# The first heads of a fused attention and soft-MoE kernel: how the first row of maxima travels, and what order the start-up work stands in

## The chip, the cores and the metric

One Trainium2 chip, one of its cores. The metric is device microseconds of one execution, the median of several runs. A profiled execution shows every instruction of the core's engines: PE (matrix products), PEld (its weight loads), DVE (VectorE), ACT (ScalarE), POOL (GpSimd), SP (which issues most transfers), and 16 DMA engines that carry the transfers.

## The reference

Attention over 4 x 8 heads of 768 positions and 64 dimensions, in which a query sees only the keys with its own hash bucket, and then a soft mixture of experts on the result:

```
q_bits = (einsum('bhsd,dk->bhsk', q, proj) > 0); k_bits likewise     # 6 bits each
mask   = q_bucket[:, :, :, None] == k_bucket[:, :, None, :]
scores = where(mask, (q @ k^T) / sqrt(64), -1e9)
attn   = softmax(scores);  attn_out = attn @ v
x      = attn_out as [3072, 512];  logits = x @ phi                  # 32 slots
slots  = softmax over tokens (logits)^T @ x; per expert relu(. @ w1) @ w2
out    = softmax over slots (logits) @ that
```

All values are 32-bit floats.

## The kernel before

The 32 heads go through one software pipeline, in pairs that share a load. For a pair, `load` brings q and k, transposed, into `raw` (two transfers of 384 KB; one buffer, so the next pair's load waits until this one has been read). `split_hi` (ACT) writes a rounded copy of `raw` into `w4` and `split_lo` the rest beside it, so that one product over 128 rows adds the high and low parts. `bits` multiplies `raw` by the projection and turns the signs into rows `bt` that push scores of unequal buckets far down. `w4` and `bt` also have one buffer each.

A head's operands are put together in one of three tiles `XY0`, `XY1`, `XY2` (names XY_133, XY_134, XY_135 in the order lists below) by transfers from SBUF to SBUF, all called `move`: `spread_y` (384 KB, the high parts of Y), `spread_bits` (four small ones from `bt`), `spread_l` (192 KB), `spread_x` (384 KB and 192 KB). The first head of all writes its Y rows directly. `first_y` zeroes some rows of a tile on GpSimd and sends rows of ones into it.

For each head `smax` (12 products, smx) finds the maximum of every query's row with 9 reductions on DVE; `shift` makes the shift `mz` of them (three tiny DVE operations m, mz, mz); `shift_rows` turns it into a row, row 64 of X and Y; `scores` (24 products, st) computes the scores again, with that row inside, and ACT takes their exponential into three tiles `pt`; `acc` (GpSimd) sums them, `av` multiplies them by v (24 products). Heads overlap: while head h is in `scores`, head h+1 is in `smax`.

`shift_rows` for every head but the first: PE transposes `mz` in one product, ACT copies the 12 x 128 result to `mr`, and SP sends it by one small transfer into row 64 of X and Y. For the first head, 24 products of one row each put the values on partition 64, and ACT and DVE copy them into the tile.

`keep_warm` issues products whose result nobody reads.

The order is a list, not a scheduler's choice: each step is entered by `at(when, f, ...)` with a time in slots, `WHEN` holds the times relative to a head, `FIRST` overrides single steps by absolute time, and the list is sorted. Each engine then runs its instructions in that order. SP's queue is in order too: a transfer that waits for its data holds up all that stand behind it.

Of the kernel before, what the change touches and what calls it, by code (L numbers as in the profile page):

```python
# [9 lines left out]
F32 = mybir.dt.float32  # L10
F32R = mybir.dt.float32r
AF = mybir.ActivationFunctionType
ALU = mybir.AluOpType
# [5 lines left out]
P = 128  # L19
NT = S // P  # L20
# [11 lines left out]
ROW = 64  # L32
# [39 lines left out]
 'batch_share': 27.6,  # L72
 'load_weights': 4.18}

FIRST = {('load', 4): 4.476,
 ('bits', 2): 1.288,
 ('split_hi', 2): 0.833,
 ('split_lo', 2, 0): 1.029,
 ('split_lo', 2, 1): 2.366,
 ('spread_y', 2): 1.587,  # L80
 ('spread_bits', 2): 1.668,
 ('spread_l', 2): 2.667,
 ('spread_x', 2): 3.34,
 ('smax', 1, 0, 0): -1.746,
 ('smax', 1, 0, 1): -1.169,
 ('smax', 1, 1, 0): 0.452,
 ('smax', 1, 1, 1): 0.57,
 ('smax', 1, 2, 0): 1.478,
 ('smax', 1, 2, 1): 1.593,
 ('smax', 1, 3, 0): 2.035,  # L90
 ('smax', 1, 3, 1): 2.061,
 ('smax', 1, 4, 0): 2.241,
 ('smax', 1, 4, 1): 2.696,
 ('smax', 1, 5, 0): 2.774,
 ('smax', 1, 5, 1): 3.433,
 ('one_sum', 30): 189.395,
 ('one_log', 30): 188.431,
 ('one_fold', 3): 189.992,
# [49 lines left out]
def lsh_attention_soft_moe(  # L148
# [11 lines left out]
    nc = tc.nc  # L160
# [35 lines left out]
    st = [dict() for _ in range(BH)]  # L196
# [21 lines left out]
    load(0)  # L218
    nc.sync.dma_start(out=pre[:, C_ID + 64:], in_=cst[:, C_ID:C_FD])
    phs = cp.tile([P, H, NS], F32, name="phs")  # L220
    for a in range(2):
        nc.sync.dma_start(out=phs[a * D:(a + 1) * D], in_=phi.rearrange("(h d) s -> d h s", d=D))

# [6 lines left out]
    ident = ident_r.bitcast(F32)  # L230
# [9 lines left out]
    p_st = ps_stack.enter_context(tc.tile_pool(name="p_st", bufs=3, space=PSUM))  # L240
    p_av = ps_stack.enter_context(tc.tile_pool(name="p_av", bufs=1, space=PSUM))
    p_mi = ps_stack.enter_context(tc.tile_pool(name="p_mi", bufs=2, space=PSUM))
    names = {p_sm: "smx", p_st: "st", p_mi: "mi"}
# [23 lines left out]
    def first_y(i):  # L267
        for ts in (Ys, Xs):
            nc.gpsimd.memset(ts[i][64:96].bitcast(F32), 0.0)
        for ts in (Ys, Xs)[i == 0:]:  # L270
            nc.gpsimd.dma_start(out=ts[i][ROW:ROW + 1, 1].bitcast(F32), in_=row)

# [16 lines left out]

    def split_lo(h, x):  # L290
        w = st[h]["w4"]
        (nc.vector if h else nc.gpsimd).tensor_tensor(out=w[:, 2 * x + 1], in0=st[h]["raw"][:, x], in1=w[:, 2 * x], op=ALU.subtract)  # L292

    def move(dst, src, eng=nc.sync):

        eng.dma_start(out=dst.bitcast(F32), in_=src.bitcast(F32))  # L296
# [10 lines left out]
    def spread_l(h):  # L307
        s = st[h]
        r = 64 * (h % 2)
        move(s["Y"][96:128], s["w4"][r:r + 32, 1:3])  # L310


    def spread_x(h):
        s = st[h]
        s["X"] = Xs[h % N_Y]
        r = 64 * (h % 2)
        move(s["X"][0:64], s["w4"][r:r + 64, 0::3])
        move(s["X"][96:128], s["w4"][r + 32:r + 64, 1:3])

    def over(out, pt, rows):  # L320
        nc.vector.tensor_scalar(out=out, in0=pt[rows, 0:HC], scalar1=con[rows, C_TH:C_TH + 1],  # L321
# [66 lines left out]

    def shift_rows(h):
        s = st[h]  # L390
        if h == 0:
            for t0, n in ((0, 4), (4, 2)):
                cols = slice(t0 * P, (t0 + n) * P)
                r = ROW
                for o, x, pool, copy in ((0, s["X"], p_mi, nc.scalar.copy),
                                         (NT, s["Y"], p_st, nc.vector.tensor_copy)):
                    pt = pool.tile([P, 512], F32, name=names[pool])
                    for t in range(n):
                        nc.tensor.matmul(pt[r:r + 1, t * P:(t + 1) * P], s["mz"][:, o + t0 + t:o + t0 + t + 1], ident,
                                         start=True, stop=True)  # L400
                    copy(x[r:r + 1, 0, cols], pt[r:r + 1, 0:n * P])
            return
        pt = p_mi.tile([P, 512], F32, name="mi")
        nc.tensor.transpose(pt[0:2 * NT, 0:P], s["mz"], ident)  # L404

        mr = mp.tile([2 * NT, P], F32R, name="mr", bufs=1)
        nc.scalar.copy(mr, pt[0:2 * NT, 0:P])  # L407
        move(s["XY"][ROW:ROW + 1, 0].rearrange("o y (t p) -> o (y t) p", p=P), mr)
# [306 lines left out]
    def at(when, f, *args):  # L715
        key = (f.__name__, *(a for a in args if isinstance(a, int)))
        plan.append((FIRST.get(key, when), len(plan), (f, *args)))

    first_y(0)
    for i in range(1, N_Y):  # L720
        at(-NT - 5 + i, first_y, i)
    at(-14, keep_warm, 10, True)
    at(-6.5, bits_rest)
    at(-13.9, bits_copy)
    at(-11, copy_ident)
    at(-2.6, keep_warm, 3, True)
    at(-2, keep_warm, 3, True)
    for h in range(BH):
        s0, x = NT * h, h % 2
        if x == 0:  # L730
            if h > 0:
                at(s0 + WHEN["load"], load, h)
            at(s0 + WHEN["bits"], bits, h)
            at(s0 + WHEN["split_hi"], split_hi, h)
            for n in range(2):
                at(s0 + WHEN["split_lo"][n], split_lo, h, n)
        for n, f in enumerate((spread_y, spread_bits, spread_l, spread_x)):
            at(s0 + WHEN["spread"][x][n], f, h)
        at(s0 + WHEN["load_v"][x], load_v, h)
        for n in range(2 * NT):  # L740
            at(s0 + WHEN["smax"][x][n], smax, h, n // 2, n % 2)
            at(s0 + WHEN["scores"][x][n], scores, h, n // 2, n % 2)
        at(s0 + WHEN["shift"][x], shift, h)
        at(s0 + WHEN["shift_rows"][x], shift_rows, h)
        for j in range(NT // 2):
            lone = h == BH - 1 and j == NT // 2 - 1
# [19 lines left out]
    last, h = NT * BH, BH - 1  # L766
# [62 lines left out]
    for x in range(2):  # L829
        pt = p_mi.tile([P, 512], F32, name="mi")[:, 0:2 * P]  # L830
        for k in range(2):
            nc.tensor.matmul(pt[:, k * P:(k + 1) * P], run_x[:, (2 * x + k) * P:(2 * x + k + 1) * P], fold,
                             start=True, stop=True)
# [176 lines left out]
```

## Time and profile before

| | us |
|---|---|
| median of 3 runs (523.57 to 529.93) | 524.46 |
| the profiled execution's own time | 524.46 |
| its span, first to last instruction | 522.4 |

The profiled execution took as long as the median run; 2.06 us of its time lie around the span. Mean granted TensorE clock over the span: 0.987 of full speed. In the page's lines a row is start, duration, engine, line, operation, output <- input, count, and in brackets how long the engine had been idle and what released it. In tables by stretch, each engine has its busy time, then come the granted clock (PEclk, 1.00 is full speed), the busy share of the DMA engines and GB/s.

### The profile page before, as it was taken

What the parts mean: (1) busy time and instruction counts of PE and PEld (TensorE: products, weight loads), DVE (VectorE), ACT (ScalarE), POOL (GpSimd) and SP (SyncE); (2) the same over time, 40 slices, a digit from 0 to 9 for tenths busy, and PEclk for the clock granted to TensorE, in tenths of its full rate; (3) what the DMA queues carried; (4) which work ended last, traced back from release to release, by engine and by line L of the source; (5) the groups of instructions that cost most, each with busy time, mean ns of one, the idle gap of its engine ahead of it and who ended that gap; (6) DMA issues with size and microseconds to landing.
All of it is one profiled execution on the core that took longest, in us unless ns stands there. A gap on an engine that the chain in (4) does not pass through costs nothing.

```text
span 522.4 us, 9095 instructions
## 1 busy us (share of the span) xinstructions
PE 499.2 (96%) x3164; PEld 284.3 (54%) x3164; DVE 369.3 (71%) x703; ACT 246.6 (47%) x463; POOL 326.8 (63%) x223
## 2 busy tenths in 40 slices
PE   7968999999999999999999999999999999999992
PEld 4544555555555555556554555565555555553562
DVE  6574877787878787777787788787777885464233
ACT  4144536464646454545454545454644545422232
POOL 9246767676739776767488785856588767411200
PEclk9789999999999999999999999999999999999998
DMA  5747475758585657575765757676636366879967
GB/s 126 188 98 188 116 196 173 193 168 197 169 197 168 178 143 203 152 210 143 217 149 167 183 175 178 188 181 182 146 101 154 73 156 234 319 286 352 410 275 293
DMA packets 39777, 99.59 MB, mean 191 GB/s; under 512 B 7458, under 2 KB 13732, under 8 KB 39732
## 3 DMA queue, kind: packets, MB, share of 16 engines
q1 hardware_dynamic: 39540, 98.94, 66.3%
q8 instruction: 25, 0.41, 0.3%
q14 instruction: 20, 0.16, 0.1%
q0 software_dynamic: 192, 0.08, 0.1%
HBM read 52.76 MB, written 6.29 MB: 113 GB/s over the span
## 4 chain that ended last, share of the span: by engine, by line
PE 70%; DVE 10%; SPq 7%; DMA 6%; POOL 2%; issue 2%; ACT 1%; DVEq 0%; ACTq 0%; POOLq 0%
PE st L421 20%; PE av L449 19%; PE smx L370 13%; SPq L296 7%; DMA XY<-bt 4%; PE qs L933 3%; DVE w L292 3%; PE qh L851 3%; DVE mx L376 3%; PE mi L461 2%; PE mi L476 2%; POOL acc L438 1%; PE mi L328 1%; DMA w<-w 1%; DMA XY<-w 1%
## 5 line engine op out<-in xcount | busy, mean ns | idle before, releaser
L438 POOL TENSOR_TENSOR acc<-acc,pt 128x768 f32<-128x768 f32 x125 | 238.8, 1911 | 39.4 <-ACT pt L425 27.1
L425 ACT ACTIVATE pt<-st 128x512 f32<-128x512 f32 x288 | 162.0, 595 | 97.2 <-PE st L421 90.8
L421 PE MATMUL st<-XY 128*128 128x512 f32 (+1 forms) x768 | 183.7, 347 | 0.0
L376 DVE TENSOR_REDUCE mx<-smx 128x1 f32<-128x512 f32 x192 | 130.8, 687 | 54.1 <-PE smx L370 53.8
L449 PE MATMUL av<-pt,v 128*64 128x384 f32 x768 | 145.3, 499 | 0.0
L370 PE MATMUL smx<-XY 96*128 96x512 f32 (+1 forms) x384 | 126.6, 375 | 9.9 <-DVE mx L376 5.4
L421 PEld LDWEIGHTS st<-XY 128*128 128x128 f32 x768 | 123.7, 191 | 21.1 <-issue 10.6
L370 PEld LDWEIGHTS smx<-XY 96*128 96x128 f32 x384 | 70.1, 191 | 74.4 <-DVE mx L376 26.1
L432 POOL TENSOR_TENSOR acc<-pt 128x768 f32<-128x768 f32 x32 | 58.6, 1830 | 63.8 <-ACT pt L425 63.8
L449 PEld LDWEIGHTS av<-pt,v 128*64 128x64 f32 x768 | 46.5, 136 | 62.7 <-issue 57.5
L373 DVE TENSOR_REDUCE mx<-smx 128x2 f32<-128x512 f32 x96 | 65.6, 683 | 4.3 <-PE smx L370 4.1
L292 DVE TENSOR_TENSOR w<-raw,w 128x768 fp32r<-128x768 f32 x30 | 41.2, 1373 | 3.7 <-ACT w L288 3.7
L468 DVE RECIPROCAL sm<-sm 128x128 f32<-128x128 f32 x45 | 39.6, 910 | 0.0
L288 ACT CAST w<-raw 128x768 fp32r<-128x768 f32 x32 | 25.1, 831 | 19.5 <-DMA XY<-w 9.7
L453 ACT COPY avs<-av 128x384 f32<-128x384 f32 x32 | 15.3, 478 | 37.2 <-PE av L449 37.2
L407 ACT CAST mr<-mi 12x128 fp32r<-12x128 f32 x31 | 7.9, 255 | 49.2 <-PE mi L404 44.6
L321 DVE TENSOR_SCALAR bt<-mi,con 128x384 fp32r<-128x384 f32 x15 | 10.1, 677 | 25.3 <-DMA XY<-bt 9.6
L607 POOL TENSOR_TENSOR dl<-lacc,dl 64x384 f32<-64x384 f32 x3 | 3.0, 999 | 25.6 <-ACT dl L606 25.6
L513 DVE TENSOR_TENSOR xq<-mi,r 128x256 f32<-128x256 f32 x45 | 17.3, 412 | 0.4 <-PE mi L511 0.4
L328 PE MATMUL mi<-raw,pb 128*32 128x384 f32 x128 | 15.2, 517 | 0.1
L933 PE MATMUL qs<-w 128*32 128x256 f32 x232 | 15.2, 382 | 0.0
L511 PE MATMUL mi<-ident,avs 128*128 128x128 f32 x90 | 14.8, 273 | 0.0
(173 smaller groups left out, 339.4 us busy)
## 6 DMA issues: line engine op xcount, KB each, us to landing
w<-w SPq DMA_DIRECT2D x61, 512.0 KB
XY<-w SPq DMA_DIRECT2D x63, 384.0 KB
raw<-qk SPq DMA_DIRECT2D x32, 384.0 KB
XY<-w SPq DMA_DIRECT2D x64, 192.0 KB
v<-vt SPq DMA_DIRECT2D x32, 192.0 KB
out<-w SPq DMA_DIRECT2D x12, 512.0 KB
xq<-w SPq DMA_DIRECT2D x3, 512.0 KB
XY<-bt SPq DMA_DIRECT2D x62, 19.5 KB
```

Source lines behind the costliest of these rows:

```text
L292: (nc.vector if h else nc.gpsimd).tensor_tensor(out=w[:, 2 * x + 1], in0=st[h]["raw"][:, x], in1=w[:, 2 * x], op=ALU.subtract)
L296: eng.dma_start(out=dst.bitcast(F32), in_=src.bitcast(F32))
L370: nc.tensor.matmul(pt[:, o:o + b - a], s["Y"][0:96, 0, t * P:(t + 1) * P], s["Y"][0:96, 1, a:b], start=True, stop=True)
L373: nc.vector.tensor_reduce(out=mx[:, n - 1:n + 1], in_=pt.rearrange("p (a x) -> p a x", a=2), axis=AX.X, op=ALU.max)
L376: nc.vector.reduce_max(out=mx[:, n:n + 1], in_=pt, axis=AX.X)
L421: nc.tensor.matmul(pt[:, o:o + b - a], x[:, 1, i * P:(i + 1) * P], x[:, 0, a:b], start=first, stop=not first)
L425: nc.scalar.activation(s["P", i // 2][:, 512 * u:512 * u + 512], pt, AF.Exp, scale=D ** -0.5)
L432: nc.gpsimd.tensor_tensor(out=s["acc"], in0=pr[:, 0:S], in1=pr[:, S:2 * S], op=ALU.add)
L438: eng.tensor_tensor(out=s["acc"], in0=s["acc"], in1=pr[:, a * S:(a + 1) * S], op=ALU.add)
L449: nc.tensor.matmul(s["av"][64 * c:64 * c + 64, 0:HC], s["v"][:, i, :], pr[:, o + c * HC:o + (c + 1) * HC], start=(i == 0), stop=(i == NT - 1))
L468: nc.vector.reciprocal(out=rs[:, k * P:(k + 1) * P], in_=rs[:, k * P:(k + 1) * P])
L933: nc.tensor.matmul(po[32 * j:32 * j + 32], hTs[g][:, f, 32 * j:32 * j + 32], wt[1, x, 2 * g + f // 4, j][:, (f % 4) * HM:(f % 4 + 1) * HM] ...
```

## The change

Four things, all in the first two pairs of heads; from the third pair on every engine runs the same instructions in the same order.

- The first head's row is transposed, copied to `mr` and sent by SP as for the other heads. The 24 one-row products and four copies go, and two groups of three `keep_warm` products.
- The second head's `smax` stands ahead of the first head's `scores`, instead of alternating with them; the third head's last parts stand later.
- GpSimd's queue issues the first head's `spread_l` and `spread_x` (three moves, 768 KB), which SP issued; `split_lo` of the second pair goes from DVE to GpSimd; the second and third heads' rows of ones come later.
- The second pair's `load` stands behind the second head's moves, and these behind the first head's row; `bits`, `split_hi` and the spreads of the second pair move to match.

```diff
-FIRST = {('load', 4): 4.476,
- ('bits', 2): 1.288,
- ('split_hi', 2): 0.833,
...
+ ('load', 2): -1.8,
+ ('spread_l', 1): -2.05,
+ ('spread_x', 1): -2.1,
...
     def first_y(i):
         for ts in (Ys, Xs):
             nc.gpsimd.memset(ts[i][64:96].bitcast(F32), 0.0)
+
+    def first_rows(i):
         for ts in (Ys, Xs)[i == 0:]:
             nc.gpsimd.dma_start(out=ts[i][ROW:ROW + 1, 1].bitcast(F32), in_=row)
...
-        (nc.vector if h else nc.gpsimd).tensor_tensor(out=w[:, 2 * x + 1], in0=st[h]["raw"][:, x], in1=w[:, 2 * x], op=ALU.subtract)
+        (nc.vector if h > 2 else nc.gpsimd).tensor_tensor(out=w[:, 2 * x + 1], in0=st[h]["raw"][:, x], in1=w[:, 2 * x], op=ALU.subtract)
...
-        move(s["Y"][96:128], s["w4"][r:r + 32, 1:3])
+        move(s["Y"][96:128], s["w4"][r:r + 32, 1:3], nc.sync if h else nc.gpsimd)
...
-        move(s["X"][0:64], s["w4"][r:r + 64, 0::3])
-        move(s["X"][96:128], s["w4"][r + 32:r + 64, 1:3])
+        eng = nc.sync if h else nc.gpsimd
+        move(s["X"][0:64], s["w4"][r:r + 64, 0::3], eng)
+        move(s["X"][96:128], s["w4"][r + 32:r + 64, 1:3], eng)
...
     def shift_rows(h):
         s = st[h]
-        if h == 0:
-            for t0, n in ((0, 4), (4, 2)):
-                cols = slice(t0 * P, (t0 + n) * P)
-                r = ROW
-                for o, x, pool, copy in ((0, s["X"], p_mi, nc.scalar.copy),
-                                         (NT, s["Y"], p_st, nc.vector.tensor_copy)):
-                    pt = pool.tile([P, 512], F32, name=names[pool])
-                    for t in range(n):
-                        nc.tensor.matmul(pt[r:r + 1, t * P:(t + 1) * P], s["mz"][:, o + t0 + t:o + t0 + t + 1], ident,
-                                         start=True, stop=True)
-                    copy(x[r:r + 1, 0, cols], pt[r:r + 1, 0:n * P])
-            return
...
     first_y(0)
+    first_rows(0)
     for i in range(1, N_Y):
         at(-NT - 5 + i, first_y, i)
+        at((-12.5, -3.52)[i - 1], first_rows, i)
     at(-14, keep_warm, 10, True)
     at(-6.5, bits_rest)
     at(-13.9, bits_copy)
-    at(-11, copy_ident)
-    at(-2.6, keep_warm, 3, True)
-    at(-2, keep_warm, 3, True)
+    at(-12.52, copy_ident)
```

SP's transfers before, from the second head's first move on (raw is the second pair's load here, bt the bits, v the first head's v; XY_135 is the third head's tile):

```order
L296 DMA XY_134<-w_155 64x2x768
L296 DMA XY_133<-w_155 32x2x768
L201 DMA raw<-qk 128x768 x2
L296 DMA XY_134<-bt 13x384 x2
L296 DMA XY_134<-bt 12x384 x2
L296 DMA XY_133<-w_155 64x2x768
L296 DMA XY_133<-w_155 32x2x768
L296 DMA XY_134<-w_155 64x2x768
L296 DMA XY_134<-w_155 32x2x768 x2
L278 DMA v_87<-vt 128x384
L296 DMA XY_135<-w_278 64x2x768
```

And now, to the same place (mr is the first head's row):

```order
L309 DMA XY_134<-w_153 64x2x768
L309 DMA XY_134<-bt 13x384 x2
L309 DMA XY_134<-bt 12x384 x2
L309 DMA XY_133<-mr 1x12x128
L309 DMA XY_134<-w_153 64x2x768
L309 DMA XY_134<-w_153 32x2x768 x2
L291 DMA v_87<-vt 128x384
L211 DMA raw<-qk 128x768 x2
L309 DMA XY_135<-w_292 64x2x768
```

The load moved from ahead of the second head's bits to behind that head's moves, the row stands ahead of those moves, and the first head's three moves are gone from this queue.

PE's products from the last maxima of the first head on, before (XY_133 is the first head, XY_134 the second):

```order
L370 MATMUL smx<-XY_133 128x512
L249 MATMUL av<-pt_83,ones 32x128 x3
L399 MATMUL mi<-ident,mz 1x128 x4
L399 MATMUL st<-ident,mz 1x128 x4
L399 MATMUL mi<-ident,mz 1x128 x2
L399 MATMUL st<-ident,mz 1x128 x2
L249 MATMUL av<-pt_83,ones 32x128 x3
L370 MATMUL smx<-XY_134 128x512
L370 MATMUL smx<-XY_134 128x256
L421 MATMUL st<-XY_133 128x512 x2
```

And now, from the same product:

```order
L384 MATMUL smx<-XY_133 128x512
L384 MATMUL smx<-XY_134 128x512
L384 MATMUL smx<-XY_134 128x256 x2
L406 MATMUL mi<-ident,mz 12x128
L384 MATMUL smx<-XY_134 128x512 x2
L384 MATMUL smx<-XY_134 128x256 x2
L384 MATMUL smx<-XY_134 128x512 x2
L423 MATMUL st<-XY_133 128x512 x2
```

The transposition of the shift stands behind the second head's first two maxima tiles, and that head's tiles run ahead of the first head's scores.

POOL's work before, from the second tile's zeroing to the first sum:

```order
L269 MEMSET XY_134 32x2x768 x2
L271 DMA XY_134<-acc_84 1x16x48 x2
L292 ISA
L292 TENSOR_TENSOR w_155<-raw,w_155 128x768 x2
L265 CAST ident<-pt_82 128x128
L269 MEMSET XY_135 32x2x768 x2
L271 DMA XY_135<-acc_84 1x16x48 x2
L432 TENSOR_TENSOR acc_84<-pt_81 128x768
```

And now:

```order
L280 MEMSET XY_134 32x2x768 x2
L305 ISA
L305 TENSOR_TENSOR w_153<-raw,w_153 128x768 x2
L276 CAST ident<-pt_82 128x128
L284 DMA XY_134<-acc_84 1x16x48 x2
L309 DMA XY_133<-w_153 32x2x768
L309 DMA XY_133<-w_153 64x2x768
L309 DMA XY_133<-w_153 32x2x768
L280 MEMSET XY_135 32x2x768 x2
L284 DMA XY_135<-acc_84 1x16x48 x2
L305 TENSOR_TENSOR w_292<-raw,w_292 128x768 x2
L434 TENSOR_TENSOR acc_84<-pt_81 128x768
```

The rows of ones moved behind the subtraction, three moves stand ahead of the third tile's zeroing, and the second pair's subtraction ahead of the first sum.

More of the change, by code (lines that the diff above doesn't have):

```diff
@@ L73 @@
  'load_weights': 4.18}
-FIRST = {('load', 4): 4.476,
- ('bits', 2): 1.288,
- ('split_hi', 2): 0.833,
[L78 to L95, printed above, removed]
+FIRST = {('smax', 2, 2, 1): 5.76,
+ ('smax', 2, 2, 0): 5.75,
+ ('smax', 2, 1, 1): 5.7,
+ ('smax', 2, 1, 0): 5.66,
+ ('smax', 2, 0, 1): 5.65,
+ ('smax', 2, 0, 0): 5.6,
+ ('load', 2): -1.8,
+ ('spread_l', 1): -2.05,
+ ('spread_x', 1): -2.1,
+ ('spread_x', 0): -12.04,
+ ('load', 4): 4.476,
+ ('bits', 2): 3.4,
+ ('split_hi', 2): 3.3,
+ ('split_lo', 2, 0): 3.45,
+ ('split_lo', 2, 1): 3.46,
+ ('spread_y', 2): 3.5,
+ ('spread_bits', 2): 3.6,
+ ('spread_l', 2): 4.2,
+ ('spread_x', 2): 4.3,
+ ('smax', 1, 0, 0): -2.3,
+ ('smax', 1, 0, 1): -2.29,
+ ('smax', 1, 1, 0): -2.28,
+ ('smax', 1, 1, 1): -2.1,
+ ('smax', 1, 2, 0): -2.05,
+ ('smax', 1, 2, 1): -2.0,
+ ('smax', 1, 3, 0): -1.99,
+ ('smax', 1, 3, 1): -1.9,
+ ('smax', 1, 4, 0): -1.8,
+ ('smax', 1, 4, 1): 0.62,
+ ('smax', 1, 5, 0): 0.63,
+ ('smax', 1, 5, 1): 1.2,
  ('one_sum', 30): 189.395,
```

## The prediction

> **What bounds the kernel now.** I read the page's first part, then busy time by stretches of the start, then the chain of waits backwards from where the start ends.
>
> ```profile
> PE 499.2 (96%) x3164; PEld 284.3 (54%) x3164; DVE 369.3 (71%) x703; ACT 246.6 (47%) x463; POOL 326.8 (63%) x223
> 9.00:21.70 12.70, 10.74 (x49) 6.13 (x49) 7.97 (x15) 1.32 (x3) 7.44 (x7) 0.73 0.69 171
> 21.70:30.00 8.30, 4.69 (x27) 2.99 (x26) 4.60 (x8) 3.63 (x6) 0.58 (x1) 1.00 0.50 116
> 30.00:39.40 9.40, 8.20 (x37) 5.37 (x37) 8.22 (x13) 2.90 (x6) 4.97 (x4) 0.82 0.64 126
> 39.40:51.00 11.60, 9.97 (x57) 5.02 (x57) 4.62 (x9) 4.41 (x9) 8.84 (x5) 1.00 0.82 193
> 51.00:62.00 11.00, 11.00 (x59) 6.63 (x59) 9.82 (x15) 6.99 (x12) 6.83 (x5) 1.00 0.56 152
> 62.00:88.00 26.00, 26.00 (x156) 15.15 (x155) 19.79 (x36) 13.62 (x25) 18.58 (x11) 1.00 0.66 176
> ```
>
> PE is busy for 96% of the span, and from 51.00 on for all of it: 11.00 of 11.00 us, then 26.00 of 26.00. The order there is the same before and after. So the question is one number: **when does PE start the product that began at 51.00**, the first maxima of the fourth head? What that product gains, the end should gain, one for one. Even all of PE's idle time from 9.00 to 51.00 (12.70 - 10.74 + 8.30 - 4.69 + 9.40 - 8.20 + 11.60 - 9.97 = 8.4 us) is 1.6% of 524.46.
>
> The chain up to it (start, duration, what):
>
> ```profile
> 20.75 5.81 DMA XY<-w
> ...
> 26.78 0.84 ACT w L288
> ...
> 43.02 2.34 SPq L296
> ...
> 47.02 3.84 DMA XY<-bt
> ...
> 51.00 0.47 PE smx L370
> ```
>
> The fourth head's bits decide 51.00; they are the last of a long stream of transfers. Earlier, the second pair's `split_hi` (26.78) waited until all moves out of the one buffer `w4` had landed. SP's queue with the times, and the speed of transfers in four stretches:
>
> ```profile
> 7.89 3.51 SPq L296 DMA_DIRECT2D XY<-w  x2
> 13.46 3.33 SPq L296 DMA_DIRECT2D XY<-bt  x4
> 28.37 0.65 SPq L296 DMA_DIRECT2D XY<-w  x1
> 29.26 3.41 SPq L296 DMA_DIRECT2D XY<-bt  x4
> 32.72 2.13 SPq L296 DMA_DIRECT2D XY<-w  x3
> 37.42 0.80 SPq L296 DMA_DIRECT2D XY<-mr  x1
> 38.27 0.50 SPq L278 DMA_DIRECT2D v<-vt  x1
> ...
> 9.00:11.10 2.10, 1.17 (x4) 0.60 (x4) 1.60 (x3) 0.38 (x1) 2.10 (x2) 1.00 0.90 189
> 14.00:16.30 2.30, 2.19 (x7) 1.27 (x7) 1.87 (x4) 0.00 (x0) 2.30 (x4) 0.50 0.86 333
> 39.40:47.70 8.30, 8.30 (x46) 4.53 (x45) 4.62 (x9) 4.16 (x8) 5.62 (x4) 1.00 0.98 232
> 39.40:49.40 10.00, 9.97 (x57) 5.00 (x56) 4.62 (x9) 4.41 (x9) 7.24 (x5) 1.00 0.89 211
> 30.70:33.40 2.70, 2.70 (x10) 2.17 (x10) 2.51 (x4) 0.60 (x2) 1.07 (x2) 0.50 0.50 95
> ```
>
> A move alone runs at 189 GB/s (9.00 to 11.10), a load at 333, and from 39.40 to 47.70 the DMA engines were 98% busy at 232 with a mixture: that stretch is bound by transfers. A move's bytes start 1.1 us after its issue (7.89, data from 9.0). SP was idle from 34.85 (32.72 + 2.13) to 37.42, waiting for the second head's row, with the third pair's load behind it.
>
> **The change part by part.** First POOL and DVE:
>
> ```profile
> 1.51 2.69 POOL L269 MEMSET XY<- 32x1536 f32 x2
> 8.87 3.70 POOL L292 TENSOR_TENSOR w<-raw,w 128x768 fp32r<-128x768 f32 x2
> 12.86 2.69 POOL L269 MEMSET XY<- 32x1536 f32 x2
> 15.50 1.00 POOL L271 DMA_DIRECT2D XY<-acc  x2
> 32.85 3.70 POOL L438 TENSOR_TENSOR acc<-acc,pt 128x768 f32<-128x768 f32 x2 [1.63 <-issue]
> 466.32 0.61 POOL L817 DMA_DIRECT2D fold<-cst  x1 [13.44 <-DMA w<-w]
> ...
> 2.83 1.40 DVE L228 COPY con<-pt 128x3 f32<-128x3 f32 x1
> 10.19 0.71 DVE L321 TENSOR_SCALAR bt<-pt,con 128x384 fp32r<-128x384 f32 x1
> 16.78 0.17 DVE L383 TENSOR_SCALAR mz<-m 128x6 f32<-128x6 f32 x1
> 34.75 1.82 DVE L383 TENSOR_SCALAR mz<-m 128x6 f32<-128x6 f32 x1
> ```
>
> *POOL.* The two row transfers ahead of the subtraction go, so it starts about 1.00 us sooner than 8.87 and ends at 11.6; the cast (12.57 to 12.86 in the rows, 0.3) ends at 11.9, the rows of ones at 12.9. No move of this size is issued from POOL before. The nearest rows are 0.50 (15.50, two in 1.00) and 0.61 (128 partitions, 466.32); upwards, SP's moves when its queue is full took up to 1.8 us each, below 0.5 there is no row. I take 0.61: three end at 14.75. Their 0.79 MB land by about 18.2 (0.79 MB / 189 GB/s after a start at 14.0), 3 us before the first scores need them. Then the third tile is zeroed from 14.75 to 17.45.
>
> *The shift.* `mz` reaches DVE at 16.78 as before, but now beside that zeroing. The two slow rows show the price: the copy at 2.83 ended at 4.23 with POOL's zeroing (1.51 + 2.69 = 4.20), and `mz` at 34.75 ended at 36.57 with POOL's additions (36.55); without POOL, it took 0.17. So I put its end at 17.5 instead of 16.95, the last operation's at 17.7. Were a move on POOL 1.8 us, the zeroing would begin after `mz` and this 0.6 us would go; at 0.5 it is 0.3 us less. The Trainium skill, "SBUF — State Buffer", section "Who interferes with whom", has the rule: a tensor_scalar in a two-port mode and a GpSimd instruction shut each other out for a whole instruction. It speaks against this part of the change; the trace agrees (1.82 against 0.17 us). By the rule the sum is 523.4 as below, without it 522.8.
>
> *The row and SP.*
>
> ```profile
> 17.29 1.87 PE L399 MATMUL mi<-ident,mz 128*1 128x128 f32 x8
> 35.23 0.50 PE L370 MATMUL smx<-XY 96*128 96x512 f32 x1
> 36.83 0.27 PE L404 MATMUL mi<-ident,mz 128*12 128x128 f32 x1 [1.10 <-DVE mz L385]
> 37.14 0.26 ACT L407 CAST mr<-mi 12x128 fp32r<-12x128 f32 x1 [3.14 <-PE mi L404]
> ```
>
> The second head's bits are now next in SP's queue when `bt` is done (10.19 + 0.71 = 10.90): four issues, 3.33 us, to 14.25. The landing: the third head's bits ended issue at 32.67 and its maxima began at 35.23, 2.56 us later (an upper bound if something else released them). So the second head's maxima start at 16.8, where 21.68 stood before: the 24 one-row products (17.29, 1.87 for the first eight) and the warm-up groups are gone. Two tiles at half clock, about 1 us, to 17.8; the transposition at 17.8, ACT 0.31 later, SP 0.28 after that (rows 36.83, 37.14, 37.42): **the row is issued at 18.4, until 19.2**. Behind it wait the second head's three moves, v and the second pair's load: queued behind a wait that the queue did not have. They start at 19.25, their bytes at 20.35: 0.79 MB of moves at 189 and 0.98 MB of v and load at 333 are 4.2 + 2.9 = 7.1 us, to 27.5 (at the mixed 232 GB/s, 7.6).
>
> Before, that load was there for `bits` at 23.87, and what counted was `split_hi` at 26.78. Now its first half comes at about 26.3 and its second at 27.5, and ACT's second half of `split_hi` ends at 28.35: the next move goes out at 28.4, where 28.37 stood. The gain up to here is nothing: the saved products were replaced by the load.
>
> *The second pair's bits.* PE at 27.5, `bt` on DVE to 28.7, issue after the move from 29.1 to 32.5 (before 32.67). The third head's maxima start at 35.1 (before 35.23).
>
> *The stream behind them.* Now the second head's row follows directly. Its `mz` stands beside the second pair's subtraction on POOL (27.45 + 3.70 = 31.15), so it ends at about 31.2, and the row is ready at 32.2: no wait at 32.5. Then v (33.3), the third head's three moves, the third pair's load, the fourth head's moves, with no gap where SP idled for 2.6 us before. From 34.4: 1.77 MB of moves and 0.98 MB of loads are 9.4 + 2.9 = 12.3 us, to 46.7; at 232 GB/s, 11.9, to 46.3. I take 46.6, against 47.70 before: **1.1 us sooner**. The bits behind it kept 3.3 us to 51.00, so the product starts at 49.9.
>
> *Does PE get there in time?* From 35.1, five tiles at DVE's pace to 37.7, then the stretch that took 10.00 us (39.40 to 49.40, the same products): 47.7. PE waits 2.2 us for the bits. That is the cover of all else I cost at nothing: the subtraction at 1.85 us on POOL instead of DVE, the sums behind it on POOL (first one at 31.2 instead of 29.42, in one row then), PE's pause for the second shift (29.5 to 31.2), and a half-speed clock after such pauses, at most 1.4 us (half of the 2.7 us at 0.50 from 30.70 on). If the transfers were faster, these would come through.
>
> Sum: 51.00 - 49.9 = 1.1 us; 524.46 - 1.1 = 523.4, the profiled execution and the median of the runs being the same number.
>
> **The rivals.**
>
> 1. *PE is the bound, not the stream.* If transfers from two queues and without SP's pauses end 2.2 us earlier than I say, the product starts when PE arrives, at 47.7: 521.2. For it: the gaps in SP's queue go. Against: 98% DMA share at 232 GB/s.
> 2. *Slower: the row waits for GpSimd's moves.* The second head's bits are issued (to 14.25) just when POOL's 0.79 MB start. If they land behind those bytes, at 18.2 + 1.0 = 19.2 instead of 16.8, the transposition, which stands behind two maxima tiles, moves from 17.8 to 20.2, and SP with the load and everything behind it by 2.3 us net: 523.4 + 2.3 = 525.7. From 1.1 us of such delay on, the change is a loss. For it: those bits landed 3.84 us after the start of the last issue (47.02) where a move stood beside them. Against: two queues. The Trainium skill, "DMA: Bandwidth & Descriptors", section "Queues, rings and completion order", says that a DMA engine takes turns between queues packet by packet; by that the bits pass the moves and this rival falls to nothing. No run here has two large queues at once, so it keeps its chance.
> 3. *The change does what it says and nothing comes of it.* The stream ends at 47.7 as before, since `split_hi` starts no earlier (28.4 against 28.37) and mixed traffic loses what the gap gave: 524.5.
>
> **How the numbers follow.** Forecast 523.4 (522.4 to 524.2) 0.47; PE-bound 521.2, 0.15; row late 525.7, 0.20; nothing 524.5, 0.15; beyond 2% either way 0.015 each. The likeliest gives 523.4. The range, 521.0 to 526.0, takes in the rivals at 521.2 and 525.7 and the runs' own scatter of a few tenths; what is left out is a worse delay of the row or a gain beyond PE's own pace. 2%, some 10 us, is about what a measurement of this kernel can tell from no change; more than all idle time of the start, so faster 0.015, same 0.97, slower 0.015.
>
> **What would show it.** Right: the first row's transfer near 18.4; the second pair's load landed near 27.5; `split_hi` of it ending near 28.4; bits of the third head issued to 32.5; no gap in SP's queue from there to the fourth head's bits; the fourth head's first maxima at 49.9 after about 2 us of idle PE, and PE full from there. Wrong: the second head's maxima starting after 18 (rival 2); that product released by PE's own order (rival 1); `mz` at 0.17 us beside POOL; or PE idle again between 51 and 88, in which case the shift is not carried to the end.

## The result and the profile after

| | before | after |
|---|---|---|
| median of 20 runs each (us) | 525.26 (521.76 to 529.93) | 528.59 (526.07 to 531.34) |
| ratio, with 95% interval | | 1.0064 (1.0041 to 1.0088) |
| span of the profiled execution, granted clock | 522.4, 0.987 | 527.2, 0.980 |

The change made the kernel 0.64% slower, 3.3 us by the medians. The forecast was 1.1 us faster, with a range up to 526.0. Here and below the ratio is worked out from the fast executions of both kernels on one chip, and need not equal the quotient of the medians.

After, the page's busy times, and five stretches of the start (the same columns as before):

```profile
PE 497.1 (94%) x3129; PEld 281.9 (53%) x3129; DVE 366.0 (69%) x699; ACT 245.9 (47%) x462; POOL 332.0 (63%) x228
...
9.00:21.70 12.70, 6.95 (x17) 3.69 (x15) 9.29 (x15) 0.70 (x2) 9.22 (x12) 0.59 0.46 100
21.70:30.00 8.30, 7.93 (x25) 5.57 (x24) 4.76 (x8) 2.57 (x5) 0.00 (x0) 0.60 0.76 194
30.00:39.40 9.40, 6.01 (x30) 2.61 (x29) 3.93 (x6) 4.21 (x8) 8.07 (x5) 1.00 0.39 92
39.40:51.00 11.60, 10.93 (x59) 5.51 (x59) 5.50 (x11) 4.21 (x8) 8.65 (x6) 1.00 0.94 223
51.00:62.00 11.00, 9.15 (x50) 6.06 (x50) 7.67 (x12) 6.05 (x11) 6.32 (x4) 1.00 0.46 96
```

PE has 2.1 us less work in all, as the one-row products are gone. Yet it is idle for 5.75 us in the first stretch (2 before), runs the second at a clock of 0.60 (1.00 before) and is idle for 1.85 us after 51.00, where nothing was lost before, all of it before the product that now starts at 52.84. DMA share in the third stretch is 0.39 where it was 0.64: SP waits there for the second pair, until 31.97.

SP's queue (bt are bits, mr the first head's row, raw the second pair's load):

```profile
11.87 3.31 SPq L309 DMA_DIRECT2D XY<-bt  x4
21.44 0.73 SPq L309 DMA_DIRECT2D XY<-mr  x1
22.27 2.67 SPq L309 DMA_DIRECT2D XY<-w  x3
24.98 0.94 SPq L291 DMA_DIRECT2D v<-vt  x1
25.97 1.52 SPq L211 DMA_DIRECT2D raw<-qk  x2
31.97 0.65 SPq L309 DMA_DIRECT2D XY<-w  x1
32.76 3.55 SPq L309 DMA_DIRECT2D XY<-bt  x4
```

The chain of waits, start, duration, what:

```profile
14.47 4.86 DMA XY<-bt
19.33 0.38 issue
19.71 1.19 PE smx L384 x3
20.91 0.23 PE mi L406
21.16 0.26 ACT mr L409
21.44 0.73 SPq L309
...
27.04 4.05 DMA raw<-qk
...
50.29 2.31 DMA XY<-bt
52.60 0.25 issue
52.84 0.47 PE smx L384
```

The second head's bits are issued until 15.18 (11.87 + 3.31; the chain counts from 14.47, the start of the last issue) and are the chain's transfer until 19.33, 4.15 us after the end of their issue. The row stands behind that head's first two maxima tiles, so it goes out at 21.44, and the three moves, v and the second pair's load stand behind the row. The load is the chain's transfer until 31.09, and the fourth head's first product, 51.00 in the profile of before, starts at 52.84.

What stands beside those bits, on POOL and on DVE:

```profile
7.98 3.58 POOL L305 TENSOR_TENSOR w<-raw,w 128x768 fp32r<-128x768 f32 x2
12.87 1.70 POOL L309 DMA_DIRECT2D XY<-w  x3
14.61 2.69 POOL L280 MEMSET XY<- 32x1536 f32 x2
...
9.94 1.84 DVE L335 TENSOR_SCALAR bt<-pt,con 128x384 fp32r<-128x384 f32 x1
17.95 0.17 DVE L397 TENSOR_SCALAR mz<-m 128x6 f32<-128x6 f32 x1
```

GpSimd issues its 0.79 MB from 12.87 to 14.57, just as the bits go out; and `bt` was done at 11.78, 0.88 us later than before. It met GpSimd's subtraction in both kernels. The subtraction has two parts of about 1.8 us. Here `bt` started at 9.94, in the second part, and ended 0.22 us after it (7.98 + 3.58 = 11.56); in the profile of before it started at 10.19, in the first part (8.87 to about 10.7), and ended 0.2 us after that one, at 10.90.

### The profile page after: what moved, and what is told of

Read it like the earlier page. It is cut to its first block, busy times and chain, and to the rows that moved or that the text cites. A ratio compares the mean times of both kernels' runs of the same rounds, so it can differ in the third digit from the quotient of the medians.

```text
span 527.2 us, 9032 instructions
## 1 busy us (share of the span) xinstructions
PE 497.1 (94%) x3129; PEld 281.9 (53%) x3129; DVE 366.0 (69%) x699; ACT 245.9 (47%) x462; POOL 332.0 (63%) x228
## 4 chain that ended last, share of the span: by engine, by line
PE 72%; SPq 9%; DMA 8%; DVE 5%; issue 2%; POOL 1%; ACT 1%; DVEq 0%; ACTq 0%; POOLq 0%
PE st L423 20%; PE av L451 20%; PE smx L384 13%; SPq L309 8%; DMA XY<-bt 4%; PE qs L935 3%; PE qh L853 3%; PE mi L463 2%; PE mi L478 2%; DVE w L305 2%; DMA raw<-qk 2%; DVE mx L390 1%; DMA w<-w 1%; PE mi L513 1%; PE mi L342 1%
## 5 line engine op out<-in xcount | busy, mean ns | idle before, releaser
L384 PE MATMUL smx<-XY 96*128 96x512 f32 (+1 forms) x384 | 128.2, 383 | 15.8 <-DMA XY<-bt 8.8
L423 PEld LDWEIGHTS st<-XY 128*128 128x128 f32 x768 | 124.5, 191 | 21.4 <-issue 10.6
L305 DVE TENSOR_TENSOR w<-raw,w 128x768 fp32r<-128x768 f32 x28 | 39.0, 1394 | 0.3 <-DMA v<-vt 0.3
L515 DVE TENSOR_TENSOR xq<-mi,r 128x256 f32<-128x256 f32 x45 | 17.3, 411 | 0.4 <-PE mi L513 0.4
L305 POOL TENSOR_TENSOR w<-raw,w 128x768 fp32r<-128x768 f32 x4 | 7.2, 1806 | 13.0 <-ACT w L301 12.9
## 6 DMA issues: line engine op xcount, KB each, us to landing
XY<-bt SPq DMA_DIRECT2D x62, 19.5 KB
```

The costliest lines, as they stand in the source:

```text
L305: (nc.vector if h > 2 else nc.gpsimd).tensor_tensor(out=w[:, 2 * x + 1], in0=st[h]["raw"][:, x], in1=w[:, 2 * x], op=ALU.subtract)
L384: nc.tensor.matmul(pt[:, o:o + b - a], s["Y"][0:96, 0, t * P:(t + 1) * P], s["Y"][0:96, 1, a:b], start=True, stop=True)
L423: nc.tensor.matmul(pt[:, o:o + b - a], x[:, 1, i * P:(i + 1) * P], x[:, 0, a:b], start=first, stop=not first)
```

## The experiments

Each is the changed kernel with one edit, unless it says otherwise, beside the kernel before on the same chip (524.6 to 525.3 us there). "The product" is the fourth head's first maxima product. Theories: **B**, the bits land late because GpSimd's moves are under way, and row and load follow; **the load**, its place behind the row costs the time; **the clock**, PE's half speed after its waits does.

**The load ahead of the row.**

```
- ('load', 2): -1.8,
+ ('load', 2): -4.0,
```

> The changed kernel with one step moved: the second pair's load stands behind the second head's bits and ahead of the first head's row in SP's queue, instead of behind that head's moves. Theory Q (the load waits in the queue for the late row, and that wait is what was lost): the load lands near 19 instead of 31.1, the second pair's split_hi then waits only for the moves, third head's maxima near 35 instead of 37.65, the fourth head's first product near 50.2 instead of 52.84, about 2.6 us less than the changed kernel, so 0.1% above to level with the kernel before. Rival B (the DMA engines' bytes bound the start, whatever the order): the same bytes have to go, the fourth head's product stays within 0.7 us of 52.8.

530.46 us, ratio 1.0110 (1.0077 to 1.0142): no better. SP's load, PE's scores with the second pair's bits (mi<-raw), and the second stretch:

```profile
15.30 2.86 SPq L211 DMA_DIRECT2D raw<-qk  x2
...
27.77 2.91 PE L423 MATMUL st<-XY 128*128 128x512 f32 x10
30.61 0.85 PE L342 MATMUL mi<-raw,pb 128*32 128x384 f32 x8
...
21.70:30.00 8.30, 7.92 (x23) 5.74 (x24) 4.95 (x8) 2.02 (x4) 0.00 (x0) 0.52 0.54 119
```

The load went out 10.7 us sooner (15.30 for 25.97), but PE's queue holds the bits behind the first head's scores, and those ran at a clock of 0.52. The load's place alone is no lever; the product came at 53.98, later than either theory of that run had it.

**Warm PE.**

```
+    at(-2.6, keep_warm, 10, True)
```

> The changed kernel with ten warm-up products of 128 columns in PE's wait ahead of the second head's maxima (17 to 19.7). Theory C (the clock, 0.59 and 0.60 up to 30 us, is what was lost): the granted clock is full by about 21, the two tiles and the transposition ahead of the row take 0.6 us less, the row at 20.8, product near 52.2. Rival Q: PE's speed is hidden behind the load's landing (31.1), product within 0.3 us of 52.8.

528.49 us, ratio 1.0086 (1.0056 to 1.0116). The second and the fourth stretch, and PE's bits of the second pair:

```profile
21.70:30.00 8.30, 5.63 (x25) 3.71 (x25) 4.92 (x8) 2.79 (x5) 0.00 (x0) 1.00 0.77 194
39.40:51.00 11.60, 11.54 (x43) 5.96 (x45) 5.23 (x8) 3.35 (x7) 6.29 (x4) 0.71 0.93 232
...
30.75 1.80 PE L342 MATMUL mi<-raw,pb 128*32 128x384 f32 x8 [2.85 <-DMA raw<-qk]
```

The clock is 1.00 as wished, and PE then waits 2.85 us for the load. Up to there, what the clock gained was lost to the load. Then the clock fell again, to 0.50 from 40 to 46 us (stretches of 2 us), and the product came at 53.64 without a wait.

**GpSimd's moves later**, behind the third tile's zeroing.

```
- ('spread_x', 0): -12.04,      # and spread_l likewise, from -12.047 to -3.51
+ ('spread_x', 0): -3.505,
```

> The changed kernel with GpSimd's three moves of the first head behind the zeroing of the third tile (issue about 16 instead of 12.9), so that they do not run while the second head's bits are in flight. Theory P (the bits landed 4.2 us after their issue because GpSimd's 0.79 MB stood beside them): bits land near 17.7 instead of 19.3, the first head's row is issued near 19.9 instead of 21.44, fourth head's first product near 51.3, 1.5 us less than the changed kernel. Rival B: the moves' bytes then run beside the second head's moves, the load still lands near 31, product within 0.5 us of 52.8. Rival: bits land late without that traffic too (19.3), then something else holds them.

The queues of POOL and SP, and PE:

```profile
16.79 1.71 POOL L309 DMA_DIRECT2D XY<-w  x3
...
12.15 3.31 SPq L309 DMA_DIRECT2D XY<-bt  x4
19.00 0.73 SPq L309 DMA_DIRECT2D XY<-mr  x1
24.52 1.50 SPq L211 DMA_DIRECT2D raw<-qk  x2
...
17.04 1.37 PE L384 MATMUL smx<-XY 96*128 96x512 f32 x3 [0.21 <-DVE mx L387]
50.97 0.47 PE L384 MATMUL smx<-XY 96*128 96x512 f32 x1 [0.22 <-PE st L423]
```

**Theory B holds.** The bits were issued later than in the changed kernel (to 15.46, not 15.18) and had landed by 17.04, in 1.58 us at most after the end of their issue and not 4.15; PE no longer waits for them, the row goes out 2.4 us sooner, and the product starts at 50.97. The time stayed at 528.11, ratio 1.0074 (1.0048 to 1.0099): that profile lost its time later, which the runs below take up.

**The second tile's rows ahead of the subtraction**, so that the subtraction starts as late as before and `bt` waits for its first part, not its second.

```
-        at((-12.5, -3.52)[i - 1], first_rows, i)
+        at((-13.95, -3.52)[i - 1], first_rows, i)
```

> The changed kernel with the second tile's rows of ones sent ahead of GpSimd's subtraction, as in the kernel before. Theory L (the subtraction, 1 us sooner, now holds DVE's bits operation: 1.84 us from 9.94 instead of 0.71 from 10.19): that operation ends near 10.8 instead of 11.78, the bits are issued 1 us sooner, the row and all behind it too: row near 20.4, product near 51.8, 1.0 us less. Rival B: product within 0.4 us of 52.8.

The bits went out from 11.00, the row at 19.48, the product came at 50.97; 527.24 us, ratio 1.0051 (1.0023 to 1.0079). Two edits that let the second head's bits land sooner thus bring the product to the place it had in the profile of before, but not the time. So two things were still unknown: what that place is worth, and where the rest goes.

**The kernel before and the changed kernel once more.**

> The kernel before, unchanged, timed against itself and profiled a second time. Theory S (the two stalls of about one microsecond near 157 to 167 us and the later ones on the bits of a head scatter from execution to execution): this profile may show some of them too, and its span then lies 2 to 3 us above the first one's. Theory T (something in the changed program makes them): this profile has no stall of TensorE above 0.5 us between 62 and 490 us, as the first had none, and the time ratio is 1.000 within its interval.

> The kernel before, profiled a third time. TensorE should again arrive at the fourth head's first product at about 49, and its bits land between 49 and 51, as in the two profiles (51.00 and 49.16); from the third head to the end a loss between 0 and 5 us against the first profile. Time ratio 1.000 within its interval.

> The changed kernel unchanged, profiled a second time. In its first profile 3.1 us were lost between the third head and the end, against the first profile of before; in the second profile of the kernel before itself 3.1 us were lost there too. Theory S (that loss scatters from execution to execution): another amount here, between 0 and 5 us, with stalls at other places. What does not scatter: the first head's row at about 21.4, the second pair landed at about 31, the fourth head's first product not under 52. Time 528.3, as in the first runs.

Before: 526.27 (1.0007, 0.9971 to 1.0043) and 523.94 (0.9972, 0.9941 to 1.0004). After: 529.35 (1.0070, 1.0035 to 1.0104). The product in the second and third profile of before, and in the second of after, where the fourth stretch stands below it:

```profile
49.16 0.47 PE L370 MATMUL smx<-XY 96*128 96x512 f32 x1 [0.27 <-DMA XY<-bt]
...
48.09 0.42 PE L370 MATMUL smx<-XY 96*128 96x512 f32 x1
...
53.17 0.47 PE L384 MATMUL smx<-XY 96*128 96x512 f32 x1
39.40:51.00 11.60, 11.07 (x45) 5.78 (x47) 5.87 (x11) 3.83 (x7) 6.09 (x4) 0.77 0.94 237
```

So **51.00 was the latest of three**: the kernel before starts its product at 49.4 on average (51.00, 49.16, 48.09), the changed one at 53.0 (52.84, 53.17). The difference, 3.6 us, is about the loss in the medians. In the second profile of after the product waited for nothing: PE itself was late, at a clock of 0.50 from 38 to 44 us. And the part behind the product isn't rigid. From the issue of the fourth head's row to PE's last instruction, in the trace:

| profile | row | PE's end | between |
|---|---|---|---|
| before, three times | 62.91, 60.88, 59.81 | 513.7, 514.8, 512.2 | 450.8, 453.9, 452.4 |
| after, twice | 64.58, 65.20 | 518.5, 522.3 | 453.9, 457.1 |

The same program takes 3 us more or less there, as theory S has it. But it is not all scatter: both profiles of the changed kernel have 2.1 us of PE's stalls between 156 and 168 us, the three of before 0.4. By the means of these few profiles that part is 3.1 us longer after the change (455.5 against 452.4), and the profiled executions differ by 6.8 us, twice the medians' 3.3; the second one of after, 533.05 us, was the slowest of its 12. So that the product's shift equals the loss is no proof that it makes it.

**Where the scatter comes from.** Two edits on the rows-first kernel tried whether PSUM banks or SP's count of transfers make the later stalls:

> The changed kernel with the second tile's rows ahead of the subtraction (whose start is level with before and whose time was 527.2), and three small products ahead of the first head's row that use one buffer of the mixed PSUM pool and two of the scores' pool: as many as the first head's row used before, so that every later tile falls on the PSUM bank that it had before. Theory P (the banks' rotation makes the later stalls): time 525, no stall of over 0.5 us in the profile after 62 us. Otherwise: 527 as without it, with the stalls near 157 to 167 us.

> The same kernel as the PSUM one without its products, and with two small loads of 1 KB on SyncE's queue at about 27 us, behind the second pair's load, so that SyncE issues as many transfers as before and each later one has the place in the rotation of its completion semaphores that it had before. Theory D (that place, or the place in the queue, makes the bits land late): time 525 and no stall over 0.5 us on bits after 62 us. Otherwise: 527 as without it, with the stalls near 157 to 167 us.

527.10 (1.0026, 0.9991 to 1.0061) and 528.30 (1.0060, 1.0024 to 1.0096): neither brings the time to 525, although both profiles lack the stalls near 160 that the rows-first kernel has. (The profiled execution of the second, 525.46 us, was the fastest of its 12.) The rows-first kernel (first two lines, DVE and POOL) and the one with two loads (last two) show what makes one of them:

```profile
160.23 1.93 DVE L305 TENSOR_TENSOR w<-raw,w 128x768 fp32r<-128x768 f32 x1
159.52 4.31 POOL L440 TENSOR_TENSOR acc<-acc,pt 128x768 f32<-128x768 f32 x2
...
159.62 0.94 DVE L311 TENSOR_TENSOR w<-raw,w 128x768 fp32r<-128x768 f32 x1
159.63 5.12 POOL L446 TENSOR_TENSOR acc<-acc,pt 128x768 f32<-128x768 f32 x2
```

DVE's subtraction takes 0.94 us if it starts 0.01 us ahead of GpSimd's sums, and 1.93 if it starts behind one. Of the 26 such subtractions after 60 us, 9, 11 and 9 took over 1.4 us in the three profiles of before, 10 and 11 in those of after; most others took 0.95. The same happens in the start: these two kernels run the same instructions up to there, but `bt` came at 10.60 in the PSUM one and took 2.07 us, waiting for the second part of GpSimd's subtraction, and at 10.44 in the other, where it took 0.49; their rows went out at 21.56 and 19.43, their products at 53.42 and 51.11.

**The second pair as before**, on the rows-first kernel: its load behind the second head's bits, and its bits, copies, moves and the third head's maxima where the kernel before has them.

```
- ('load', 2): -1.8,
+ ('load', 2): -4.0,
- ('bits', 2): 3.4,
+ ('bits', 2): 1.288,
...
- ('smax', 2, 0, 0): 5.6,
```

> The changed kernel with the second tile's constant rows ahead of the subtraction, and with one part of the change undone: the second pair is fetched right behind the second head's bits, and its bits, copies, moves and maxima stand at the places they had in the kernel before, among the first head's scores. The row, the second head's maxima ahead of its scores and GpSimd's moves and subtractions stay as changed. Theory F (what the change costs is the second pair's late fetch): the third head's first maxima start near 31 instead of 36 to 38, TensorE arrives at the fourth head's first product at about 49 as in the two profiles of before (49.4 and 48.9) instead of 50.6, and the time is level with before, 525. Theory R (the row and the maxima ahead cost it): TensorE arrives at 50.5 or later, time 527.

**The same with the rows left late**, which completes the square of the two parts:

> The changed kernel with only the second pair's fetch and placing undone; the second tile's rows stay behind the subtraction, so that the second head's bits are again written late, at 11.8, and land late, and the row goes out at about 21.4 as in the changed kernel. It completes the square of the two parts (row late or not, pair late or not). If the two costs add up: TensorE at the fourth head's first product at about 50, time 525.5 to 526.5, so 1 to 1.5 us of the loss is the late row and 2 to 3 us the late pair. If the row's lateness costs only where the pair is late as well: 524.6, level with before.

The second head's maxima, the second pair's bits and the product, first with the rows early, then late:

```profile
17.80 1.19 PE L378 MATMUL smx<-XY 96*128 96x512 f32 x3 [2.28 <-DMA XY<-bt]
25.80 1.51 PE L336 MATMUL mi<-raw,pb 128*32 128x384 f32 x8
50.02 0.47 PE L378 MATMUL smx<-XY 96*128 96x512 f32 x1 [1.80 <-DMA XY<-mr]
...
19.59 1.19 PE L378 MATMUL smx<-XY 96*128 96x512 f32 x3 [2.78 <-DMA XY<-bt]
27.59 1.51 PE L336 MATMUL mi<-raw,pb 128*32 128x384 f32 x8
50.69 0.47 PE L378 MATMUL smx<-XY 96*128 96x512 f32 x1 [0.50 <-DMA XY<-bt]
```

| second pair | row late (21.4) | row early (19.5) |
|---|---|---|
| behind the row | 1.0064 (1.0041 to 1.0088) | 1.0051 (1.0023 to 1.0079) |
| as before | 1.0042 (1.0008 to 1.0075) | 0.9990 (0.9958 to 1.0021) |

With both undone the kernel is level with before, at 524.64 us, as theory F had it (though the third head's maxima began at 33.78, not near 31). What it keeps of the change (the transposed row, the second head's maxima ahead, GpSimd's moves and subtractions) costs nothing measurable together. With one part undone the loss stays above zero, at 527.08 us with the row late, which is neither of the two times expected; how the loss divides is within the intervals. PE reaches the product (its start less its wait) at 48.2 with both undone, at 50.2 with the row late, at 50.6 with the pair late and at 50.6 with both. These are single profiles: second ones have 49.0 with the pair late (the kernel with two loads) and 53.2 with both, so they don't divide the loss either.

**The late pair alone, on the kernel before:**

```
- ('bits', 2): 1.288,
+ ('load', 2): -1.8,
+ ('bits', 2): 3.4,
...
```

> The kernel before with that one part of the change alone: the second pair's load at the place behind the first head's row, and its bits, copies, moves and maxima at the places of the changed kernel; the row itself as before. Theory F: load issued near 22.5, landed near 27.5, the third head's first maxima at 35 to 37, TensorE at the fourth head's first product at 50.5 or later, time 527 to 528. Theory R: TensorE there at about 49.5, time 525.

525.90 us, ratio 1.0011 (0.9983 to 1.0039): no measurable loss, and theory F's 527 to 528 is missed. The second pair's bits and the product:

```profile
27.77 1.16 PE L335 MATMUL mi<-raw,pb 128*32 128x384 f32 x8
50.59 0.47 PE L377 MATMUL smx<-XY 96*128 96x512 f32 x1 [1.10 <-DMA XY<-bt]
```

Here SP has no row to wait for, so the load goes out at 21.9 instead of 25.97, and PE is kept busy by the one-row products, so its clock from 21.70 to 30.00 is 1.00. So the late fetch alone costs nothing that can be measured. That it is dear behind the row's wait and on a PE at half clock fits the runs; which of the two makes it so was not separated.

**Can both be beaten?** Two tries: rows first, moves late, load ahead and ten warming products together; and the level kernel with five.

> The changed kernel with four edits together: the second tile's constant rows ahead of the subtraction, GpSimd's three moves behind the third tile's zeroing, the second pair's load directly behind the second head's bits and ahead of the first head's row, and ten warming products in TensorE's wait for that row. Theory L (each of row, load and clock hid the others): bits issued 11.0 to 14.3, the second head's maxima at about 16.5, row at about 18.9, load landed by 24, first head's scores from about 20.5 to 28 at a clock over 0.9, third head's first maxima near 33, fourth head's first product near 48.5, 2.5 us ahead of before's 51.00; time 525 if the 2 to 3 us of the later stalls stay, 522.5 if they go. Theory N (something further holds the start, for instance TensorE itself): first product of the fourth head not under 50.5, time 527.

> The kernel that was level with before (the second tile's rows ahead of the subtraction, the second pair fetched and placed as before) with five warming products in TensorE's wait for the second head's bits, between 15.5 and 17.8 us, where its clock had fallen to 0.50. Theory C (with the pair's data early nothing hides the clock any more): granted clock 1.00 from about 22 us instead of from 27.5, the first head's scores and the third head's bits 1 to 2 us sooner, TensorE at the fourth head's first product at 47 instead of 48.2, time 523.5 to 524, which would be ahead of both kernels. Theory M (transfers and VectorE set that place, as the wait of 1.80 us on a transfer there says): the product stays at 49 to 50 and the time at 524.6.

The first gave 528.07 us, ratio 1.0037 (1.0004 to 1.0070): the ten products ran until 20.04, while `mz` was ready at 17.3, so the row went out only at 21.13, the clock was back at 0.50 from 24 to 28 us, and the product came at 52.27. So no run shows what load and clock are worth together. The second gave 524.21, ratio 1.0008 (0.9978 to 1.0038), no better than before:

```profile
21.70:30.00 8.30, 6.72 (x29) 3.79 (x28) 4.18 (x9) 3.82 (x7) 2.30 (x2) 0.79 0.61 130
49.02 0.47 PE L378 MATMUL smx<-XY 96*128 96x512 f32 x1 [1.41 <-DMA XY<-bt]
```

PE arrives at 47.6 and waits 1.41 us for bits: a faster PE again runs into the transfers. No version beat the kernel before.

## Why the prediction was wrong, step by step

- **What bounds it.** The product's place did move, by 3.6 us on average, but that the time follows from it alone is not shown. Wrong to read its place from one execution: 51.00 held 1.64 us of waiting for bits that the two later profiles hardly have (0.27 and none). The stretch called bound by transfers, 39.40 to 47.70, has PE busy for 8.30 of 8.30 us as well. A gain of 1.1 us was to come out of a wait that is mostly not there.
- **The landing of the second head's bits**, the first step that failed, at 19.33 instead of 16.8. The prediction took 2.56 us from the end of their issue; it took 4.15. The other 0.9 us came from `bt`, below. This was rival 2, whose landing at 19.2 is nearly what came, in part by luck: it put the bits behind all of GpSimd's bytes, but with the pair as before, where they were issued to 14.31, they landed at 17.45, ahead of GpSimd's 384 KB move, which landed 4.7 us after its issue at 13.31. It had 0.20 because the two queues spoke against it. The Trainium skill's rule beside it ("DMA: Bandwidth & Descriptors", section "Queues, rings and completion order") has a DMA engine take turns between queues packet by packet. The trace does not contradict it: from 16 to 18.5 us, with all of these transfers issued, 109 packets of GpSimd's queue and 47 of SP's went. What failed is the conclusion that the bits pass the moves by it; 4.15 us with GpSimd's 0.79 MB under way stand against at most 1.58 without.
- **`bt` at 10.90.** It came at 11.78. The subtraction on POOL, begun 0.9 us sooner, made `bt` wait for its second part instead of its first. The prediction priced such a meeting for `mz`, beside the Trainium skill's rule in "SBUF — State Buffer", section "Who interferes with whom", and forgot to look who else stands beside the moved subtraction. `mz` itself came after the zeroing and took 0.17.
- **Row 18.4, load landed 27.5.** 21.44 and about 31.1: the queue behind the wait was named rightly, and its delay carried over in full (3.0, then 3.6 us). The three moves on POOL took 0.57 each, near the 0.61 taken.
- **PE in time, at 47.7**, the second step that failed. PE came at 50.6, and at 53.2 in the second profile. A row on time doesn't mend it: with GpSimd's moves later the row went out at 19.00, 0.6 us behind the forecast, and PE still came at 50.75. The prediction allowed 12.6 us from the third head's first maxima (35.1 to 47.7); the changed kernel took 13.0 and 14.8, the kernel before 14.1, 13.7 and 13.0. And the half clock was allowed 1.4 us, from a pause late in the start. It ran from about 12 on: the 25 products of the second stretch took 7.93 us, and 5.63 in the warmed kernel, 2.3 us less; in the second profile it came again from 38 to 44.
- **The shift is carried one for one.** In one execution it is not: 3 us of scatter lie behind the product in the kernel before, and on average it isn't shown. The expected scatter of "a few tenths" was wrong as well.
- **Rival 2's price.** 525.7 came from 51.00 - 1.1 + 2.3 = 52.2; the product was at 52.84 and 53.17. The 1.1 us of gain in the stream and the base of 51.00 made it too low.

**Open.** How the loss divides between the late row and the late pair, and whether the stretch behind the start is systematically longer in the changed kernels. Both profiles of it, and those of load ahead, moves late, rows first and the two with the pair as before and no warming, show 2.0 to 2.1 us of PE's stalls between 156 and 168; the three of before, the late pair alone and the other changed kernels have at most 0.43 there. The kernel with the moves late had its product at 50.97 in its profile, as before, and still took 528.11 us. What starts the phase that makes these stalls was not found: the two edits made for it changed other phases as well.

## What to carry to other kernels

Before costing a queue's order, ask of each small transfer that somebody waits for which bulk transfers are under way when it goes out, on other queues too: 77 KB landed 4.15 us after the end of their issue beside 0.79 MB, and at most 1.58 us after it without. Don't take the start's critical wait from one profile: where an instruction waits for a transfer, see a second execution first, since 1.6 us of the forecast's base were one execution's chance. And when an instruction moves to GpSimd or in time on it, check every DVE instruction that it will now meet.

## What the runs showed of the hardware that was not expected

- Four small transfers of SP's queue (77 KB) landed 4.15 us after the end of their issue in the changed kernel, and 3.14 in the one with the pair as before, while 0.79 MB of GpSimd's queue were under way; with these later, within 1.58 us.
- DVE's subtraction that started 0.01 us ahead of GpSimd's sums kept its 0.94 us; others took up to 2.6. With GpSimd busy for 63% of the span such meetings are many. `bt`, which came 0.16 us later in one of two kernels that run the same instructions up to it, ended 1.74 us later, and the fourth head's product 2.3 us later.
- In the changed kernel PE's clock stood at 0.50 from about 12 to 28 us, and in its second profile from about 14 to 26 (stretches of 2 us), through patchy work (busy 6.95 of 12.70 us in the first stretch); it came back to 1.00 once PE was busy without a pause, and in the second profile fell to 0.50 again from 38 to 44. Ten products in the wait for the bits had it back by 20.
